# The order of the first units in a linear-attention and gated-MLP kernel: second head pair second, shared tail third

## The chip, the cores and the metric

The kernel runs on one core of a Trainium2 chip. The core has a matrix engine (TensorE, PE in the profile, with its weight loads as PEld), a vector engine (DVE), an activation engine (ACT), a general engine (GpSimd, POOL) and a queue engine that only starts transfers (SyncE, SP). Each runs its own instructions in order. Transfers are started on three queues: SP's, ACT's and POOL's; a transfer that changes the type (fp32 in memory, bf16 on chip) is started by POOL here. The metric is the device time of one execution in microseconds (us), lower is better.

## The reference

Eight batches, eight heads, 576 tokens, head size 64, 128 features per sign:

```python
def phi(x):
    proj = einsum('bhsd,df->bhsf', x, w_phi)
    proj = proj - max(abs(proj), axis=-1, keepdims=True)
    return concatenate([exp(proj), exp(-proj)], axis=-1)
q_p, k_p = phi(q), phi(k)
kv  = einsum('bhsf,bhsd->bhfd', k_p, v)
num = einsum('bhsf,bhfd->bhsd', q_p, kv)
den = einsum('bhsf,bhf->bhs', q_p, sum(k_p, axis=2))[..., None] + 1e-06
x = num / den                     # heads side by side: (8, 576, 512)
h = maximum(x @ w_in, 0.0)        # 1024 columns: u and v
v_n = (v - mean(v)) / sqrt(var(v) + 1e-06)
v_s = einsum('ts,bsd->btd', w_spatial, v_n) + b_spatial
out = (u * v_s) @ w_out
```

## The kernel before

**Units.** Of a batch's 576 tokens, 512 are the main part and 64 the tail. The tails of two batches (a group) share one 128-row tile. The attention is cut into 36 units: for each batch four *pairs* (two heads, 512 tokens each), and for each group one *tail* unit (both batches' tails, all heads). The list `units` (L558) fixes their order. For the first group it was: pair 1 of batch 0, tail, pairs 2, 3 and 4 of batch 0, then batch 1's four (called pairs 5 to 8 here).

**Stages of a unit.** `a_transpose` (L238) puts k and q in feature order through TensorE and DVE ("next"). `a_keys` (L260) projects k by w_phi, DVE takes the maximum of each row (`mk`, L268) and ACT the two exponentials (`kf`, L271). `a_scale` (L288) makes `em`, the exponentials of that maximum on ACT (L291), and POOL multiplies v with them (`vs`, L296, two instructions, and a cast at L298). For a tail unit `tail_scale` (L306) does that per batch (`vst`, L311, L313). `a_queries` (L273) does the same maximum for q (L282) and splits it in two bf16 parts (`mhl`, L285 and L286; on DVE for units 0 to 4, on POOL later). `a_max_t` (L315, "maxima") turns that part round, and `a_qfeat` (L325, "features") makes q's exponentials (`qf`, L355). `a_kv` (L358, "sums") forms kv of a pair from its own `kf` and `vs` and from the tail's, `a_num` (L381, "attention") the quotient, and `a_x_t` (L392, "out") its transpose.

**Steps.** `step(i)` (L622) issues, for each stage in the order of `ORDER` (L599), the unit whose number plus the stage's lag is i: `LAGS` in general, `FIRST` for the pairs of batch 0, `FT` for the first tail (L604 to L615). So step i does keys and queries of unit i, transposes of unit i + 1, sums of unit i - 2, attention of unit i - 3. When a batch's last pair is through "out", that batch's MLP (`b_tasks`, L581) goes to a queue of matmul tasks that `fill` (L608) puts between the stages. For batch 0 that is in step 7. The MLP's first spatial product (`b_s`, L508, matmul L513) needs the four normalised tiles `vn` (L454), written by POOL.

**Transfers and orders.** After each step the list `io`, filled by `at` (L664), issues transfers: batch 1's k and q (`load`, L97, POOL's queue) and v (`load_v`, L101, SP's queue) after step 1, MLP weights after steps 2 to 4, later batches' k and q after steps 4 and on. `load_tail` (L109) fetches a tail. A planner orders the instructions of each engine by their inputs and their place in the program; those wrapped in `pin` (L60) stay behind the instruction that was written last on their engine. A pinned instruction is shown under L61.

**Start.** Pair 1's k and q come as fp32 by SP's queue (`first`) and are cast on DVE. All other k and q come as bf16 by POOL's queue; pair 2's with `load("k", 0, 0, 2, 2)` and the same for q, after the tail's. Before the first exponentials ACT fills `vst` and `vnt` of the even and the odd groups and casts w_phi. `weights_with_max` (L228) builds `wm` on POOL (L230 to L232, four times three instructions), which is read from unit 10 on (L334); it is written after step 7 and not pinned.

Of the kernel before, what the change touches and what calls it, by code (L numbers as in the profile page):

```python
# [8 lines left out]
FP32 = mybir.dt.float32  # L9
# [7 lines left out]
def kernel(  # L17
# [106 lines left out]
    for i in range(2):  # L124
        nc.scalar.dma_start(out=wphi_f[i * D:(i + 1) * D, :], in_=w_phi)
    alloc(0)
    first = {}
    for x, t in (("k", k), ("q", q)):
        first[x] = s2.tile([P, 2, NB * D], FP32, tag="ob", name="first", bufs=6)
        pin(nc.sync.dma_start)(out=first[x], in_=main_ap(t, 0, 0, 2))  # L130
# [14 lines left out]
    for i in range(NM):  # L145
        for tiles, name in ((mhl, "mhl"), (mT, "mT")):
# [10 lines left out]
                                 scalar2=None, op0=ALU.mult)  # L157
    for x in ("k", "q"):
        pin(nc.vector.tensor_copy)(out=half_tile(x, 0, 0)[:, 0:2], in_=first[x])
    vst, vnt = [], []  # L160
    for i in range(2):
        t = cpool.tile([P, 2, 2, H, DA], BF16, name=f"vst{i}")
        pin(nc.scalar.copy)(out=t.rearrange("p b s h d -> p (b s h d)"), in_=zero.to_broadcast([P, 4 * H * DA]))
        vst.append(t)
        if i == 0:
            for y in range(2):
                r = slice(y * D, (y + 1) * D)
                pin(nc.scalar.copy)(out=wphi2[r, y * F:(y + 1) * F], in_=wphi_f[r, :])
        t = cpool.tile([P, 2, HALF], BF16, name=f"vnt{i}")
        for bl, row in ((0, TL), (1, 0)):  # L170
            pin(nc.scalar.copy)(out=t[:, bl, :], in_=ident[:, row:row + 1].to_broadcast([P, HALF]))
        vnt.append(t)
    load_v(0)
    for x in ("k", "q", "v"):
        load_tail(x, 0)
    load("k", 0, 0, 2, 2)
    load("q", 0, 0, 2, 2)
# [50 lines left out]
    def weights_with_max():  # L228
        for j in range(0, H, 2):
            nc.gpsimd.tensor_copy(out=wm[:, j, :], in_=wphi2[:, 0:F])  # L230
            nc.gpsimd.tensor_tensor(out=wm[:, j + 1, :], in0=wphi2[:, F:2 * F], in1=sel[:, j + 1, :], op=ALU.add)
            nc.gpsimd.tensor_copy(out=wm[D:D + 2 * H, j, :], in_=sel[0:2 * H, j, :])  # L232
# [5 lines left out]
    def a_transpose(u):  # L238
# [3 lines left out]
        for x, copy in (("k", nc.vector.tensor_copy if u["i"] < EK else nc.scalar.copy), ("q", nc.vector.tensor_copy)):  # L242
            pt = psum.tile([P, 4, P], BF16, tag="bank", name="pt")
            for j in range(4):
# [4 lines left out]
                nc.tensor.transpose(out=pt[:, j, :], in_=blk, identity=ident)  # L249
# [38 lines left out]
    def a_scale(u):  # L288
# [11 lines left out]
        else:  # L300
            d = gs[u["g"]]
            d["vs"], d["unit"], d["em"] = vst[u["g"] % 2], u, em
            for bl in range(2 if u["i"] > 1 else 1):
                tail_scale(u["g"], bl)
# [252 lines left out]
    for g in range(G):  # L557
        if g > 0:  # L558
            units.append(dict(pair=False, g=g, i=len(units)))
        for b in (2 * g, 2 * g + 1):  # L560
            for pj in range(NP):
                units.append(dict(pair=True, g=g, b=b, pj=pj, i=len(units)))
                if b == 0 and pj == 0:
                    units.append(dict(pair=False, g=g, i=len(units)))
# [169 lines left out]
```

## Time and profile before

| | |
|---|---|
| median of 5 runs | 284.14 us (282.28 to 284.51) |
| the profiled execution's own time | 284.51 us |
| its span in the profile | 282.7 us |
| PE busy | 258.7 us, 92% |
| DVE, ACT, POOL busy | 230.0, 223.2, 198.9 us |
| TensorE clock granted | 0.996 |

The span runs from the first to the last instruction; what lies around it makes 1.8 us. A line of the timeline has the start, the length, the engine, the line, the operation, the tile written and the tile read, the count, and in brackets how long the engine was idle before it and what ended that. "Busy" of several instructions counts overlaps once. The matmul's ends are modelled, and a matmul of 512 columns is shown with 0.38 us while the next starts after 0.22. A wait is put down to the event that came last by the profile, which can be an innocent one where several ended together.

### The profile page before, as it was taken

What the parts mean: (1) busy time and instruction counts of PE and PEld (TensorE: products, weight loads), DVE (VectorE), ACT (ScalarE), POOL (GpSimd) and SP (SyncE); (2) the same over time, 40 slices, a digit from 0 to 9 for tenths busy, and PEclk for the clock granted to TensorE, in tenths of its full rate; (3) what the DMA queues carried; (4) which work ended last, traced back from release to release, by engine and by line L of the source; (5) the groups of instructions that cost most, each with busy time, mean ns of one, the idle gap of its engine ahead of it and who ended that gap; (6) DMA issues with size and microseconds to landing.
All of it is one profiled execution on the core that took longest, in us unless ns stands there. A gap on an engine that the chain in (4) does not pass through costs nothing.

```text
span 282.7 us, 8167 instructions
## 1 busy us (share of the span) xinstructions
PE 258.7 (92%) x3042; PEld 172.3 (61%) x3042; DVE 230.0 (81%) x575; ACT 223.2 (79%) x504; POOL 198.9 (70%) x358
## 2 busy tenths in 40 slices
PE   3277899989999999999999999999999999999993
PEld 2046686767766577666666675666666765654441
DVE  5279999887999988998889989997889897566441
ACT  6739999997899997899889987899789977723601
POOL 8469999999758995799949984889548832420710
PEclk9999999999999999999999999999999999999998
DMA  6998999989877999979998999999665301121205
GB/s 178 208 179 103 200 210 235 145 152 189 96 95 166 176 200 203 172 184 214 154 143 126 220 262 127 202 190 235 95 122 132 85 3 48 66 77 38 111 3 185
DMA packets 85100, 41.91 MB, mean 148 GB/s; under 512 B 52098, under 2 KB 80450, under 8 KB 85060
## 3 DMA queue, kind: packets, MB, share of 16 engines
q1 hardware_dynamic: 57348, 29.90, 51.7%
q0 software_dynamic: 27552, 11.41, 36.4%
q8 instruction: 24, 0.39, 0.6%
q14 instruction: 16, 0.13, 0.2%
q10 hardware_dynamic: 160, 0.07, 0.1%
HBM read 32.85 MB, written 9.44 MB: 150 GB/s over the span
## 4 chain that ended last, share of the span: by engine, by line
PE 62%; ACT 10%; DMA 9%; POOL 7%; DVE 7%; issue 3%; POOLq 0%; ACTq 0%; DVEq 0%
PE ps L513 9%; PE pv L437 9%; PE po L538 8%; PE pu L492 7%; PE ps L256 6%; DMA q_tl<-in_q_dram 4%; PE pv L368 4%; ACT kf L271 4%; PE pn L388 4%; DMA k_bf<-in_k_dram 3%; PE pq L334 3%; PE ps L514 2%; ACT qf L355 2%; DVE stats L440 2%; DVE mk L268 2%
## 5 line engine op out<-in xcount | busy, mean ns | idle before, releaser
L271 ACT ACTIVATE kf<-ps 128x512 bf16<-128x512 f32 x144 | 76.1, 633 | 11.6 <-DVE mk L268 11.1
L296 POOL TENSOR_TENSOR vs<-v_f,em 128x512 bf16<-128x512 f32 x64 | 65.5, 1045 | 21.3 <-ACT em L291 16.4
L355 ACT ACTIVATE qf<-pq 128x512 bf16<-128x512 f32 x128 | 66.6, 619 | 9.0 <-PE pq L334 8.5
L268 DVE TENSOR_REDUCE mk<-ps 128x4 f32<-128x512 f32 x72 | 47.7, 677 | 1.3 <-PE ps L256 0.4
L282 DVE TENSOR_REDUCE mq<-ps 128x4 f32<-128x512 f32 x62 | 39.8, 680 | 2.5 <-PE ps L256 2.2
L513 PE MATMUL ps<-w_spT,vn 128*128 128x512 bf16 x128 | 33.2, 379 | 0.5 <-POOL vn L454 0.4
L440 DVE BATCH_NORM_STATS2 stats<-vr 128x6 f32<-128x512 bf16 (+1 forms) x40 | 26.7, 684 | 7.2 <-ACT vr L439 6.9
L516 DVE TENSOR_TENSOR uT<-ps,uT 128x512 bf16<-128x512 f32 x32 | 22.0, 686 | 12.9 <-PE ps L514 12.8
L538 PE MATMUL po<-w_out_bf,uT 128*128 128x512 bf16 x128 | 32.3, 379 | 0.0
L492 PE MATMUL pu<-xT,w_in_bf 128*128 128x512 bf16 x128 | 32.1, 379 | 0.0
L437 PE MATMUL pv<-w_in_bf,xT 128*128 128x512 bf16 x128 | 31.5, 379 | 0.1
L439 ACT ACTIVATE vr<-pv 128x512 bf16<-128x512 f32 (+1 forms) x40 | 23.5, 615 | 7.3 <-PE pv L437 6.1
L368 PE MATMUL pv<-vs,kf 128*128 128x66 bf16 x512 | 24.6, 194 | 1.3 <-ACT kf L271 1.3
L454 POOL TENSOR_SCALAR vn<-vr,rs 128x512 bf16<-128x512 bf16 x32 | 24.4, 770 | 1.1
L379 DVE TENSOR_TENSOR x<-pn,rc 128x256 bf16<-128x256 f32 x64 | 24.9, 417 | 0.3
L388 PEld LDWEIGHTS <-qf 128*128 128x128 bf16 x512 | 20.2, 97 | 7.8 <-ACT qf L355 1.2
L368 PEld LDWEIGHTS <-kf 128*128 128x128 bf16 x512 | 22.1, 98 | 3.5 <-issue 2.3
L494 ACT ACTIVATE uT<-pu 128x512 bf16<-128x512 f32 x32 | 19.6, 639 | 4.9 <-PE pu L492 3.2
L388 PE MATMUL pn<-kv,qf 128*128 128x66 bf16 x512 | 21.9, 193 | 1.0 <-ACT qf L355 1.0
L541 ACT COPY ob<-po 128x512 f32<-128x512 f32 x18 | 11.0, 610 | 14.9 <-PE po L538 8.6
L370 PE MATMUL pv<-vst,kf 128*128 128x66 bf16 x128 | 21.2, 191 | 0.8 <-POOL vst L313 0.8
L311 POOL TENSOR_TENSOR vst<-v_tl,em 64x512 bf16<-64x512 f32 x16 | 16.3, 1039 | 7.7 <-ACT em L291 7.4
(128 smaller groups left out, 568.0 us busy)
## 6 DMA issues: line engine op xcount, KB each, us to landing
out_dram<-ob SPq DMA_DIRECT2D x32, 256.0 KB, 2.5
v_f<-in_v_dram SPq DMA_DIRECT2D x12, 512.0 KB, 6.1
k_bf<-in_k_dram POOLq DMA_DIRECT2D x15, 256.0 KB, 6.2
q_bf<-in_q_dram POOLq DMA_DIRECT2D x15, 256.0 KB, 6.7
v_f<-in_v_dram SPq DMA_DIRECT2D x2, 1024.0 KB, 12.3
qt<-qT_b SPq DMA_DIRECT2D x24, 64.0 KB, 4.2
v_tl<-in_v_dram SPq DMA_DIRECT2D x8, 128.0 KB, 5.1
w_in_bf<-in_moe_w_in_dram POOLq DMA_DIRECT2D x2, 512.0 KB, 7.6
```

What stands on the lines that cost most here:

```text
L268: nc.vector.tensor_reduce(out=u["mk"][:, hs], in_=pk, axis=AX.X, op=ALU.max, apply_absolute_value=True)
L271: nc.scalar.activation(out=u["kf"][:, s, hs, :], in_=pk, func=AF.Exp, bias=0.0, scale=sc)
L282: nc.vector.tensor_reduce(out=mq[:, 4 * half:4 * half + 4], in_=pq, axis=AX.X, op=ALU.max, apply_absolute_value=True)
L296: nc.gpsimd.tensor_tensor(out=vs[:, s, :, 0:D], in0=st[u["b"]]["v"][:, pj * H:(pj + 1) * H, :], in1=em[:, s, :].unsqueeze(2).to_broadcast( ...
L355: nc.scalar.activation(out=qf[:, s], in_=pq, func=AF.Exp, bias=0.0, scale=sc)
L368: nc.tensor.matmul(out=pv[:, hh, s, :], lhsT=u["kf"][:, s, 4 * hh + c, :], rhs=u["vs"][:, s, 4 * hh + c, :], start=(c == 0), stop=False)
L388: nc.tensor.matmul(out=pn[:, pos, :], lhsT=u["qf"][hh][:, s, pos, :], rhs=d["kv"][:, 2 * u["pj"] + hh, s, :], start=(s == 0), stop=(s == 1))
L437: nc.tensor.matmul(out=pv[r], lhsT=lhs(kc), rhs=w_in_bf[:, kc, HALF:DFF], start=(kc == 0), stop=(kc == KC - 1))
L440: nc.vector.bn_stats(out=stats[r], in_=dst[r])
L492: nc.tensor.matmul(out=pu, lhsT=w_in_bf[:, kc, dc * P:(dc + 1) * P], rhs=d["xT"][:, kc, :], start=(kc == 0), stop=(kc == KC - 1))
L513: nc.tensor.matmul(out=ps, lhsT=d["vn"][:, sp, cs], rhs=w_spT[:, sp, 0:T0], start=(sp == 0), stop=False)
L538: nc.tensor.matmul(out=po[r], lhsT=lhs(dc), rhs=w_out_bf[:, dc, :], start=(dc == 0), stop=(dc == KC - 1))
```

## The change

In the first group the units are now pair 1, pair 2, tail, pair 3, pair 4. Pair 2's k and q come as fp32 by SP's queue right behind pair 1's and are cast by two pinned POOL instructions; the two POOL loads for them are gone. POOL's loads of pairs 3 and 4 are issued behind these casts. v of batch 0 comes in two halves, with the tail's k, q and v between them. w_phi comes by one transfer that reads the weights twice, in place of two transfers.

The steps 0 to 3 follow lists of their own (`START`): features of pairs 1 and 2 come one step after their queries (before: two), sums three (before: two), attention four (before: three). The transposes of the tail and of pair 3 stand in their own step ("here", pinned) and not in the step before.

The zeros of `vst` of the odd groups are now a DVE memset, placed ahead of the first casts, and the constant rows of `vnt` of the odd groups two POOL copies after step 1; ACT casts w_phi first, then fills `vnt` and `vst` of the even groups. Batch 1's first k and q loads are issued after step 0 (before: 1). `wm` is built in two halves, pinned, after steps 6 and 7. The instructions of `tail_scale` are pinned, and the second batch's half of the first tail is scaled after step 5 (before: 4).

```diff
-    for i in range(2):
-        nc.scalar.dma_start(out=wphi_f[i * D:(i + 1) * D, :], in_=w_phi)
+    nc.scalar.dma_start(out=wphi_f, in_=bass.AP(tensor=w_phi.tensor, offset=w_phi.offset,
+                                                ap=[[0, 2], [F, D], [1, F]]))
...
-    for x, t in (("k", k), ("q", q)):
-        first[x] = s2.tile([P, 2, NB * D], FP32, tag="ob", name="first", bufs=6)
-        pin(nc.sync.dma_start)(out=first[x], in_=main_ap(t, 0, 0, 2))
+    for h0 in (0, 2):
+        for x, t in (("k", k), ("q", q)):
+            first[x, h0] = s2.tile([P, 2, NB * D], FP32, tag="ob", name="first", bufs=6)
+            pin(nc.sync.dma_start)(out=first[x, h0], in_=main_ap(t, 0, h0, 2))
...
+    vst = [cpool.tile([P, 2, 2, H, DA], BF16, name=f"vst{i}") for i in range(2)]
+    pin(nc.vector.memset)(vst[1], 0.0)
     for x in ("k", "q"):
-        pin(nc.vector.tensor_copy)(out=half_tile(x, 0, 0)[:, 0:2], in_=first[x])
-    vst, vnt = [], []
-    for i in range(2):
-        t = cpool.tile([P, 2, 2, H, DA], BF16, name=f"vst{i}")
-        pin(nc.scalar.copy)(out=t.rearrange("p b s h d -> p (b s h d)"), in_=zero.to_broadcast([P, 4 * H * DA]))
...
-    load_v(0)
+        pin(nc.vector.tensor_copy)(out=half_tile(x, 0, 0)[:, 0:2], in_=first[x, 0])
+    vnt = [cpool.tile([P, 2, HALF], BF16, name=f"vnt{i}") for i in range(2)]
+
+    def fill_vnt(i, copy):
         for bl, row in ((0, TL), (1, 0)):
+            pin(copy)(out=vnt[i][:, bl, :], in_=ident[:, row:row + 1].to_broadcast([P, HALF]))
+
+    for y in range(2):
+        r = slice(y * D, (y + 1) * D)
+        pin(nc.scalar.copy)(out=wphi2[r, y * F:(y + 1) * F], in_=wphi_f[r, :])
+    fill_vnt(0, nc.scalar.copy)
+    pin(nc.scalar.copy)(out=vst[0].rearrange("p b s h d -> p (b s h d)"), in_=zero.to_broadcast([P, 4 * H * DA]))
+    load_v(0, 0)
     for x in ("k", "q", "v"):
         load_tail(x, 0)
-    load("k", 0, 0, 2, 2)
-    load("q", 0, 0, 2, 2)
+    load_v(0, 1)
+    for x in ("k", "q"):
+        pin(nc.gpsimd.tensor_copy)(out=half_tile(x, 0, 0)[:, 2:4], in_=first[x, 2])
     load("k", 0, 1)
     load("q", 0, 1)
...
-    def weights_with_max():
-        for j in range(0, H, 2):
+    def weights_with_max(n):
+        for j in range(4 * n, 4 * n + 4, 2):
...
+                (pin(nc.tensor.transpose) if u["i"] in LATE else nc.tensor.transpose)(out=pt[:, j, :], in_=blk, identity=ident)
...
-            for bl in range(2 if u["i"] > 1 else 1):
+            for bl in range(2 if u["g"] else 1):
...
-                if b == 0 and pj == 0:
+                if b == 0 and pj == 1:
                     units.append(dict(pair=False, g=g, i=len(units)))
...
+    LATE = (2, 3)
+    START = [[(what, 0) for what in names.split()] for names in (
+        "keys next queries", "keys maxima queries features", "maxima features here keys queries",
+        "maxima here keys queries features sums next")]
+    HEAD = dict(next=-1, maxima=1, features=1, sums=3, attention=4, out=4)
...
     def lag(u, what):
-        return (FT if u["i"] == 1 else FIRST if u["pair"] and u["b"] == 0 else LAGS).get(what, 0)
+        if what == "next" and u["i"] in LATE:
+            return NU
+        if u["i"] < 5:
+            return (HEAD if u["i"] < 2 else FIRST if u["pair"] else FT).get(what, 0)
+        return LAGS.get(what, 0)
...
-    at(1, load, "k", 1, 0)
-    at(1, load, "q", 1, 0)
+    at(0, load, "k", 1, 0)
+    at(0, load, "q", 1, 0)
+    at(1, fill_vnt, 1, nc.gpsimd.tensor_copy)
...
-    at(4, tail_scale, 0, 1)
+    at(5, tail_scale, 0, 1)
...
-    at(7, weights_with_max)
+    at(6, weights_with_max, 0)
+    at(7, weights_with_max, 1)
```

## The prediction

> **What bounds the kernel now.** I read the busy time by stage first, to see where TensorE is not the limit.
>
> ```profile
> 0.00:8.00 8.00, 3.08 (x16) 1.81 (x16) 5.01 (x19) 5.71 (x7) 7.23 (x16) 1.00 0.74 189
> 8.00:20.00 12.00, 4.54 (x29) 3.16 (x29) 5.01 (x12) 6.44 (x15) 5.57 (x15) 1.00 1.29 204
> 20.00:44.00 24.00, 20.45 (x312) 16.90 (x311) 23.17 (x66) 21.83 (x53) 23.75 (x35) 1.00 1.11 170
> 44.00:70.00 26.00, 24.68 (x322) 18.04 (x322) 21.60 (x61) 23.57 (x56) 24.51 (x43) 1.00 1.25 175
> 70.00:250.00 180.00, 178.21 (x2174) 119.05 (x2172) 161.24 (x394) 156.08 (x360) 131.10 (x240) 1.00 0.91 149
> ```
>
> Columns: stage, its length, then busy us of PE, PEld, DVE, ACT, POOL, the granted clock, DMA, GB/s. From 70 to 250 us PE is busy 178.21 of 180: a delay or gain on PE ahead of 70 reaches the end whole, nothing later swallows it. The first 20 us hold only 7.6 us of PE work. From 20 to 44 POOL is full (23.75 of 24) and DVE nearly (23.17); from 44 to 70 POOL still is (24.51 of 26). So the opening has two clocks: the first loads set when work starts, and POOL sets how fast it is handed to PE.
>
> Then the PE timeline, for who starts late:
>
> ```profile
> 6.04 1.01 PE L256 MATMUL ps<-wphi,kT 128*128 128x256 bf16 x4 [0.27 <-ACT wphi L61]
> ...
> 13.13 0.58 PE L249 MATMUL pt<-ident,k_tl 128*128 128x128 bf16 x4 [5.22 <-DMA k_tl<-in_k_dram]
> ...
> 15.96 0.58 PE L249 MATMUL pt<-ident,q_tl 128*128 128x128 bf16 x4 [2.25 <-DMA q_tl<-in_q_dram]
> ...
> 24.37 0.61 PE L256 MATMUL ps<-wphi,kT 128*128 128x256 bf16 x4
> ...
> 71.19 1.03 PE L513 MATMUL ps<-w_spT,vn 128*128 128x512 bf16 x4
> ```
>
> After pair 1's projections (6.04) PE waits 5.22 and 2.25 us for the tail's k and q; pair 2 follows at 19.35, and 24.37 is pair 3's key projection. 71.19 is batch 0's first spatial matmul, which needs all four `vn`.
>
> The POOL timeline, for where it is free and what it delivers:
>
> ```profile
> 6.70 0.77 POOL L61 DMA_DIRECT2D q_bf<-in_q_dram  x1
> ...
> 12.37 2.04 POOL L296 TENSOR_TENSOR vs<-v_f,em 128x512 bf16<-128x512 f32 x2 [3.50 <-DMA v_f<-in_v_dram]
> ...
> 17.19 0.28 POOL L232 COPY wm<-sel 16x128 bf16<-16x128 bf16 x1
> 19.97 2.04 POOL L311 TENSOR_TENSOR vst<-v_tl,em 64x512 bf16<-64x512 f32 x2 [2.50 <-ACT em L291]
> ...
> 55.57 0.21 POOL L298 CAST vs<-em 128x32 bf16<-128x32 f32 x1
> ...
> 67.19 2.28 POOL L454 TENSOR_SCALAR vn<-vr,rs 128x512 bf16<-128x512 bf16 x3
> ```
>
> POOL idles 3.50 and 2.50 us, and from 19.97 runs with no gap worth naming through `vs` of pair 8 (ends 55.8) to the last `vn` (ends 69.47). PE's load of those weights starts at 71.1, so POOL has 1.65 us of slack there. The chain of waits puts 8.65 us at 39.68 on a k transfer; the matmul it ends in (L437) reads `xTt`, which DVE wrote at 47.98, so I read this as that copy and not as a load.
>
> Last, the third pair's q transfer, which POOL issues at 6.70:
>
> ```profile
> q_bf<-in_q_dram POOLq DMA_DIRECT2D x1, 256.0 KB, 15.3
> ```
>
> It lands at 22.0.
>
> **The change, part by part.** *Loads of pair 2.* Two 128 KB POOL loads go (0.79 + 0.72 us of issue), two fp32 loads join SP's queue ahead of v. On SP, k lands at 0.73 + 2.8 = 3.5 and q at 1.25 + 3.4 = 4.65; the queue then moves about 0.25 MB per us, so 0.26 MB more each gives 6.1 and 7.2. By the old rows it was 17.2 and 18.7. SP's later issues (v in halves, tail v, batch 1's v) slip by the two new issues of 0.5 us and by 0.5 MB, and the extra v issue; v of heads 0 to 3 stands at 1.57 MB of its queue, just where all of v stood, so it lands by 12.3 at the latest.
>
> *Casts on POOL.* No such row exists. A 128x128 copy takes 0.292, a 128x32 cast 0.208: 0.0009 per element, so 512 elements are 0.63; the 512-element TENSOR_SCALAR of L454 is 0.77. I take 0.7 (ends 0.63 and 1.05, the two-input row). They run at 6.1 to 8.0, in the old idle before 12.37, so they cost nothing by themselves. But pair 3's and 4's k and q loads are queued behind them: issue of the last moves from 6.70 to 8.8, done 9.6. If that cover is gone, 3 us at most pass to these loads.
>
> DVE's own cast rows of this shape are 0.54 and 0.43, so casts left there would take 1.4 us off POOL where it idles and put 1.0 on DVE; the sum is the same by either. The Trainium skill, GPSIMD Engine Reference, section 4.1, speaks against the change here: it sends elementwise work to VectorE, and its 3.1 gives 512 elements at best 769 ns on GpSimd.
>
> *Pair 3's data.* POOL's queue loses two loads ahead of these. At about 0.08 MB per us while SP's queue also moves (the rows of 13 to 18 us), 0.26 MB less is 3 us, less the later issue: 22.0 becomes about 20.0. Ends: 18.7, the landing of the load whose place it takes; 24.9, the old 15.3 us after issue at 9.6. From landing to key projection is 0.6 (18.76 to 19.35 for pair 2), so pair 3 starts at 20.6 in place of 24.37: 3.8 earlier. Pairs 1 and 2 and the tail before it fit: ACT has two exps sets more (2.1 each, pair 2's keys and queries) plus pair 1's queries, ready by 17, and the tail's at 17 to 19.4.
>
> *From pair 3 to the fill.* The same units, with the same DVE work, follow in the same steps; sums and numerators of pairs 1 and 2 keep one per step, moved by one. I keep 3.5 of 3.8 for the fuller DVE queue (bound: 4.8, ACT's start of pair 3's exps, 25.77 against 21).
>
> *ACT and DVE setup.* ACT loses one 1.95 and one 1.13 copy set; its first exps (9.95) start after w_phi (5.99), `vnt` 1.14 and `vst` 1.95, at 9.1; pair 1's `em` follows 2.2 later at 11.3. DVE gains a memset of 1,056 words: the 576-word one took 0.54, so 1.0, of which 0.66 is idle time before the first cast; the 0.35 left is covered by the wait for w_phi at 6.04. One DMA for w_phi instead of two: 4.4 us either way, up to 0.3 (PE's wait) to gain, counted as 0.
>
> *POOL's sum.* `vs` of pair 1 starts at 11.3 (ends: 11.3 by `em`, 12.4 by v). Behind it: itself 2.2; all that ran from 19.97 to 55.80, 35.8 (the moved loads and the tail's second half are in it, only in another order); `wm`, no longer in the idle stretch, 4 x (0.292 + 0.424 + 0.284) = 4.0; `vnt` of the odd groups, two copies of 0.63, 1.3 (end: 1.5 by 0.77). Together 43.3: ends at 54.6, with 0.4 of waiting for pair 3's `em`, 55.0. Before: 55.8. So POOL, which had 6 us of idle time, wins only 0.8, because 5.3 us of work were put in the full stretch. With the slack of 1.65 PE can be at L513 2.5 us earlier, not 3.5. Nothing POOL does in between binds sooner: the second half of the tail now stands behind pair 5's maxima, its end near 39 to 40.5, and sums that need it ran at 44.61, or 41.1 when 3.5 earlier.
>
> **Sum:** min(3.5, 0.8 + 1.65) = 2.5 us. The profiled run took 284.51 (span 282.7), so 282.0 against itself; its time is 0.37 above the median of the runs, 284.14, so 281.6 against that.
>
> Splitting v is a second place to weigh. The 1024 KB loads land in 12.3 at the median, the 512 KB ones in 6.1: no loss per byte, so I count nothing. v's second half is first used by pair 3's `vs` at about 23, so even some us more would stay hidden. The Trainium skill, DMA: Bandwidth & Descriptors, section Bandwidth, speaks against it: it wants batches of 1 MiB and more; an estimate by the fixed 2 us per transfer that the page fits for POOL's path would land that half 2 us later.
>
> **The rivals.** *POOL does not bind* (0.17). If the planner puts `wm` or the next group's tail products (4.5 us, ahead of the first root) behind `vn`, the whole 3.5 to 4.5 stays: about 280.2. For it: `wm` is first read at 80.15 and pair 10's sums at 78.94. Against: the pinned order puts both halves of `wm` behind loads of steps 6 and 7, ahead of `vn`.
>
> *POOL takes all of it* (0.15). v lands at 12.4, casts and `vnt` at their upper ends: 12.4 + 43.6 + 0.4 = 56.4, 0.6 later than before; with the slack 1.0 is left: 283.1, no change that can be told. For it: 12.37 was released by v and the bytes ahead of half of v are the same. Against: POOL's queue has nothing but the tail until 8.
>
> *Pair 3's loads late: slower* (0.18). At 24.9 its keys are at 25.5 and its `em` at 28.3; POOL, free at 22.9, idles 5.4 in its full stretch. 54.6 + 5.4 = 60.0, 4.2 late, less 1.65: +2.6, 286.7. It turns at an idle of 1.2 + 1.65 = 2.85 us, that is at a landing near 22.4. For it: the issues stand behind two casts that wait for SP's queue, and batch 1's loads now compete. Against: 0.26 MB less in that queue. A start as the diff has it, with no effect on the order of these engines, I exclude: nothing else feeds pair 2.
>
> **How the numbers follow.** My case 0.50, the rivals 0.17, 0.15, 0.18. 0.5% is 1.4 us, what a measurement here can tell from nothing. My own case spans 1.0 to 3.5 of gain (280.6 to 283.1), 0.43 of it beyond 1.4. Faster: 0.43 + 0.17 = 0.60. Same: 0.07 + 0.14 = 0.21. Slower: 0.18 + 0.01 = 0.19. The range takes in the second gain up to 4.8 (279.3) and the late load up to 1.5 of its 2.6 (285.6); outside lie 0.03 and 0.14.
>
> **What would show it.** Right: no wait of PE for tail loads; `first` of pair 2 landed by 7.5; pair 3's L256 near 20.6; POOL without a gap from 11 to 69; `vs` of pair 8 ending near 55; PE waiting for `vn` 1 us before its first L513, near 68.7. Wrong: a POOL gap between 20 and 30 (late loads), L513 below 67.5 (POOL not binding), or a stage after 70 whose PE idle has grown, for there the offset would not carry.

## The result, and the profile after

The changed kernel takes 285.62 us at the median against 284.33 for the one before: ratio 1.005, 95% interval 1.0038 to 1.0061. It is slower by half a per cent, where 281.6 and a gain were predicted. The ratios leave out executions in a slower state of the chip, here two of the changed kernel's 43 (291.79 and 908.68 us). The profiled execution took 285.31 (span 283.4) against 284.51 (span 282.7): 0.8 in the profile, 1.3 between the medians. Single executions of the kernel before scatter from 282.28 to 286.19, so one profile tells where time goes, and only the runs tell which kernel is faster. Lines of the code stand two further down than before: L256 is now L258, L513 is L515, L514 is L516, L454 is L456, L437 is L439, L538 is L540.

Busy time by stage after, in the columns of the first view before:

```profile
0.00:8.00 8.00, 1.21 (x8) 0.79 (x9) 4.36 (x17) 1.88 (x4) 4.56 (x12) 1.00 0.82 185
8.00:20.00 12.00, 9.27 (x66) 6.67 (x65) 8.80 (x20) 11.78 (x24) 8.76 (x13) 1.00 1.31 240
20.00:44.00 24.00, 19.28 (x316) 16.63 (x317) 23.13 (x64) 18.89 (x47) 21.92 (x35) 0.93 1.19 160
44.00:70.00 26.00, 24.67 (x313) 17.85 (x309) 21.25 (x58) 23.57 (x56) 24.11 (x48) 1.00 1.22 181
70.00:250.00 180.00, 177.32 (x2152) 117.88 (x2150) 160.37 (x392) 154.82 (x358) 133.50 (x243) 1.00 0.91 149
```

PE does 9.27 us of work between 8 and 20 where it did 4.54: the empty stretch was indeed filled. The work that was put there ran at a lower rate: four products of 128x256 took 1.06 us as late as 13.50 and 0.61 from 18.37 on (before: 1.04 as late as 20.28), though the clock column shows 1.00. But ACT, with 5.71 us of work in the first 8 before, has 1.88 now, and POOL, which was full from 20 to 44 (23.75), is idle for 2.1 us of it.

The PE timeline after, at the tail, at pair 3 and at batch 0's first spatial products:

```profile
8.02 1.01 PE L258 MATMUL ps<-wphi,kT 128*128 128x256 bf16 x4 [1.16 <-ACT wphi L61]
...
18.37 0.61 PE L258 MATMUL ps<-wphi,kT 128*128 128x256 bf16 x4 [0.30 <-DVE kT L253]
18.81 0.60 PE L258 MATMUL ps<-wphi,qt 128*128 128x256 bf16 x4
21.95 0.23 PE L319 MATMUL pt<-ident,mhl 128*128 128x128 bf16 x1 [2.54 <-DVE mhl L288]
22.02 0.39 PE L61 MATMUL pt<-ident,k_bf 128*128 128x128 bf16 x4
22.24 0.39 PE L61 MATMUL pt<-ident,q_bf 128*128 128x128 bf16 x4
22.92 0.61 PE L258 MATMUL ps<-wphi,kT 128*128 128x256 bf16 x4 [0.29 <-DVE kT L253]
...
71.21 0.39 PE L515 MATMUL ps<-w_spT,vn 128*128 128x512 bf16 x1 [0.36 <-POOL vn L456]
71.96 0.39 PE L515 MATMUL ps<-w_spT,vn 128*128 128x512 bf16 x1 [0.36 <-POOL vn L456]
72.19 0.38 PE L516 MATMUL ps<-w_spT,vnt 128*128 128x512 bf16 x1
```

The waits for tail loads are gone. Pair 3 begins at 22.92 (before 24.37), and not for want of data: its transposes (22.02) are pinned behind the tail's maxima (21.95), and these wait 2.54 us for DVE. The last two lines of L515 wait for `vn` tile by tile, so the first product of the bias rows (L516) is at 72.19. Before it was at 72.05:

```profile
72.05 0.38 PE L514 MATMUL ps<-w_spT,vnt 128*128 128x512 bf16 x1
```

The lead is spent by then.

The POOL and the ACT timeline after:

```profile
6.74 0.61 POOL L61 CAST k_bf<-first 128x512 bf16<-128x512 f32 x1 [2.21 <-DMA first<-in_k_dram]
7.81 0.61 POOL L61 CAST q_bf<-first 128x512 bf16<-128x512 f32 x1 [0.46 <-DMA first<-in_q_dram]
...
13.12 2.04 POOL L298 TENSOR_TENSOR vs<-v_f,em 128x512 bf16<-128x512 f32 x2 [3.23 <-ACT em L293]
...
26.32 2.04 POOL L298 TENSOR_TENSOR vs<-v_f,em 128x512 bf16<-128x512 f32 x2 [1.63 <-ACT em L293]
...
58.01 0.21 POOL L300 CAST vs<-em 128x32 bf16<-128x32 f32 x1
...
69.63 2.28 POOL L456 TENSOR_SCALAR vn<-vr,rs 128x512 bf16<-128x512 bf16 x3
```

```profile
6.08 1.28 ACT L61 ACT_TABLE_LOAD   x1 [6.08 <-DMA wphi_f<-in_w_phi_dram]
7.37 0.60 ACT L61 CAST wphi<-wphi_f 64x128 bf16<-64x128 f32 x2
8.00 1.14 ACT L61 COPY vnt<-ident 128x512 bf16<-128x512 bf16 x2
9.04 1.95 ACT L61 COPY vst<-zero 128x2112 bf16<-128x2112 bf16 x1
10.89 2.05 ACT L273 ACTIVATE kf<-ps 128x512 bf16<-128x512 f32 x4
```

POOL starts `vs` of pair 1 at 13.12, later than before (12.37), waits 1.63 at pair 3, ends `vs` of pair 8 at 58.2 (before 55.8) and the last `vn` at 71.91 (before 69.47). ACT's first instruction is now the w_phi cast, and the load of its function table, 1.28 us, which ran at 1.95 before, stands with it behind the w_phi transfer. ACT's timeline before:

```profile
1.95 1.28 ACT L61 ACT_TABLE_LOAD   x1 [1.95 <-issue]
3.24 1.95 ACT L61 COPY vst<-zero 128x2112 bf16<-128x2112 bf16 x1
5.10 0.29 ACT L61 CAST wphi<-wphi_f 64x128 bf16<-64x128 f32 x1
...
9.95 2.05 ACT L271 ACTIVATE kf<-ps 128x512 bf16<-128x512 f32 x4
```

After L516 the two executions run in step: from the second product of the bias rows (74.52 before, 74.50 after) to 262 us they are within 0.04. Two differences come after that, both in the last batch. ACT's last `vr` starts 0.28 later, and the end of the span comes 0.38 later after the last output products. The timeline of all engines there, its ACT lines and SP's last, first of the kernel before:

```profile
261.78 0.60 ACT L439 ACTIVATE vr<-pv 128x512 bf16<-128x512 f32 x1 [1.13 <-POOL rs L448]
262.64 0.60 ACT L439 ACTIVATE vr<-pv 128x512 bf16<-128x512 f32 x1 [0.27 <-PE pv L437]
...
278.94 1.11 SPq L553 DMA_DIRECT2D out_dram<-ob  x2
```

and of the changed kernel:

```profile
261.81 0.60 ACT L441 ACTIVATE vr<-pv 128x512 bf16<-128x512 f32 x1 [1.13 <-POOL rs L450]
262.96 0.60 ACT L441 ACTIVATE vr<-pv 128x512 bf16<-128x512 f32 x1 [0.55 <-PE pv L439]
...
279.25 1.11 SPq L555 DMA_DIRECT2D out_dram<-ob  x2
```

The last issue ends at 280.05 before and at 280.36 after, the spans at 282.7 and 283.4: 2.65 us are left in the one and 3.04 in the other. Spans are printed to 0.1 us, so such lengths up to the end are good to 0.05. So the span's 0.7 is 0.14 at L516, -0.1 on the way to 262, and 0.28 and 0.38 at the end; the last 0.1 of the profiled 0.8 lies around the span.

### The profile page after: what moved, and what is told of

It is laid out like the page before. It is cut to its first block, busy times and chain, and to the rows that moved or that the text cites. A ratio compares the mean times of both kernels' runs of the same rounds, so it can differ in the third digit from the quotient of the medians.

```text
span 283.4 us, 8170 instructions
## 1 busy us (share of the span) xinstructions
PE 259.6 (92%) x3042; PEld 173.3 (61%) x3042; DVE 232.0 (82%) x576; ACT 220.4 (78%) x501; POOL 199.6 (70%) x360
## 4 chain that ended last, share of the span: by engine, by line
PE 66%; DVE 14%; ACT 10%; POOL 3%; issue 3%; DMA 2%; POOLq 0%; ACTq 0%; DVEq 0%
PE pv L439 11%; PE ps L515 9%; PE po L540 9%; PE ps L258 8%; PE pu L494 6%; PE pv L370 5%; DVE mk L270 4%; PE pn L390 4%; ACT kf L273 4%; PE pq L336 3%; PE ps L516 2%; ACT qf L357 2%; POOL vn L456 2%; DVE stats L442 2%; DMA wphi_f<-in_w_phi_dram 2%
## 5 line engine op out<-in xcount | busy, mean ns | idle before, releaser
L515 PE MATMUL ps<-w_spT,vn 128*128 128x512 bf16 x128 | 33.8, 380 | 1.6 <-POOL vn L456 1.4
L518 DVE TENSOR_TENSOR uT<-ps,uT 128x512 bf16<-128x512 f32 x32 | 21.9, 686 | 14.5 <-PE ps L516 14.5
L540 PE MATMUL po<-w_out_bf,uT 128*128 128x512 bf16 x128 | 32.3, 379 | 0.0
L439 PE MATMUL pv<-w_in_bf,xT 128*128 128x512 bf16 x128 | 31.5, 379 | 0.2 <-ACT kf L273 0.2
L456 POOL TENSOR_SCALAR vn<-vr,rs 128x512 bf16<-128x512 bf16 x32 | 24.4, 771 | 1.1
```

The source lines that it names most:

```text
L439: nc.tensor.matmul(out=pv[r], lhsT=lhs(kc), rhs=w_in_bf[:, kc, HALF:DFF], start=(kc == 0), stop=(kc == KC - 1))
L515: nc.tensor.matmul(out=ps, lhsT=d["vn"][:, sp, cs], rhs=w_spT[:, sp, 0:T0], start=(sp == 0), stop=False)
L540: nc.tensor.matmul(out=po[r], lhsT=lhs(dc), rhs=w_out_bf[:, dc, :], start=(dc == 0), stop=(dc == KC - 1))
```

## The experiments

Theories. *POOL binds, ACT starts late* (mine, mended): POOL's work as summed, but its start and its wait at pair 3 were set wrongly. *The order holds pair 3*: its place on PE behind the tail's maxima, not its load. *The end*: the two small losses after 262 us have nothing to do with the opening.

**The start on ACT.** The fill goes first, so that the table load and 1.95 us of copies run while w_phi is on its way.

```diff
+    pin(nc.scalar.copy)(out=vst[0]..., in_=zero...)
     for y in range(2):
         pin(nc.scalar.copy)(out=wphi2[...], in_=wphi_f[r, :])
     fill_vnt(0, nc.scalar.copy)
-    pin(nc.scalar.copy)(out=vst[0]..., in_=zero...)
```

> The changed kernel, but ACT's first instruction is again the fill of vst (even groups), which needs no transfer, and the two casts of w_phi come behind it. Theory A (start): ACT's table load waited 6.08 us for w_phi because it stands in front of ACT's first instruction; now it loads at about 2 us, the casts of w_phi end near 6.7 in place of 7.97, pair 1's vs on POOL starts near 11 in place of 13.12, pair 3's keys near 21.1 (its q lands at 20.5) in place of 22.92, the last vn ends near 70.1 in place of 71.91. Time 1.8 us below the changed kernel, about 283.8, no longer slower than before. Theory B (only POOL's total of work counts, not when it starts): vn and the time move by less than 0.5 us. Theory C (the loss sits in the last 20 us of the kernel or in the clock dip at 24 to 28 us): nothing moves in the time though the start is earlier.

284.69 in the profile; 285.02 by the runs, ratio 1.0038 (1.0013 to 1.0063). `vs` of pair 1 came 2.0 us sooner (11.13, where it waited 1.01 for v), the tail's keys 0.44 (17.93), pair 3's too (22.48 for 22.92), L516 at 71.65. The start is repaired, and only 0.44 of its 2.0 us reached pair 3: something behind it held.

**wm on POOL, early.** Unpinned and after step 7, as before; it then ran at 10.3 to 14.5, in POOL's idle stretch. The second kernel has the fill first as well.

```diff
-            pin(nc.gpsimd.tensor_copy)(out=wm[:, j, :], in_=wphi2[:, 0:F])
+            nc.gpsimd.tensor_copy(out=wm[:, j, :], in_=wphi2[:, 0:F])
...
-    at(6, weights_with_max, 0)
+    at(7, weights_with_max, 0)
```

> The changed kernel, but the twelve POOL instructions that build wm are not pinned and written after step 7 as before, so that the planner puts them behind pair 4's q load, from about 9.9 us, where POOL idles. Theory A: 4.0 us leave POOL's full stretch, of which 0.9 comes back as pair 1's vs starts at 14 and not at 13.12, and that is taken from the wait of 1.63 ahead of pair 3's vs; the last vn ends near 68 in place of 71.91, PE does not wait for it and keeps its lead of 1.2 us over the kernel before; L516 first near 71.0; 1.2 us below the changed kernel, about 284.4. Theory B gives the same here. Theory C: no change in the time.

> Both edits. Theory A: pair 3's keys near 21.1, vs of pair 1 near 13.9 (wm ahead of it), the last vn near 67, L516 first near 69.1 in place of 72.19: 3 us below the changed kernel, about 282.5, 0.6% below the kernel before. Theory B: as with wm alone, 284.4. Theory C: no change.

284.93, ratio 1.0018 (0.9992 to 1.0044), and 285.07, 1.0027 (1.0000 to 1.0053). The wait for `vn` was gone in both (`vn` ends 69.85 and 69.15), as POOL's theory says, but L516 came at 72.72 and 72.02. `wm` ran ahead of the tail's products: `vst` at 23.16 in place of 21.76, pair 4's keys at 27.95 in place of 26.81, and pair 8's at 47.77 and 47.08 in place of 45.89. In these traces PE gave back what POOL won. Not all of that is the work of `wm`: in the first trace the granted clock was 0.74 from 20 to 24 us and 0.50 from 24 to 32, and that execution, at 285.87, lies 0.9 above its kernel's median. In the second the clock was 1.00 and 0.94 up to 28 us, and pair 4's keys still came 4.7 after pair 3's (23.01 and 27.72), against 3.65 with the fill first alone (22.48 and 26.13). By the runs the first kernel is 0.7 below the changed one, with intervals that just overlap, so whether relieving POOL at this place pays is not settled.

**The start on ACT, in the old order.** The kernel before with w_phi cast first.

```diff
+    for y in range(2):
+        pin(nc.scalar.copy)(out=wphi2[...], in_=wphi_f[r, :])
     vst, vnt = [], []
     for i in range(2):
...
-        if i == 0:
-            for y in range(2):
-                pin(nc.scalar.copy)(out=wphi2[...], in_=wphi_f[r, :])
```

> The kernel before with one part of the change alone: ACT casts w_phi first, ahead of its fills. Theory A: ACT's table load moves from 1.95 to about 5.7 and pair 1's keys from 6.04 to about 7.7, but PE then waits for the tail's k until 13.1 and POOL idles 2.5 us ahead of 19.97, so the old order covers all of it: within 0.3 us of the kernel before. Rival: a late first exponential costs its 1 to 2 us in the old order too, near 285.7, and the whole loss of the changed kernel is this.

285.22, ratio 1.0014 (0.9983 to 1.0045), the profile 283.72. Here ACT's table load waited until 4.01, the first exponentials came at 11.72 in place of 9.95 and `vs` of pair 1 at 13.94 in place of 12.37; yet pair 2's keys were at 18.63 (19.35) and the first product of the bias rows at 71.32 (72.05). So in the trace the late start costs nothing: pair 2 waits for the tail's loads behind it. The runs alone leave room for more, as the interval reaches 1.0045. Filling that wait took the cover away from ACT's start.

**Pair 3 ahead of the tail's maxima.**

```diff
-        "maxima here keys queries features sums next")]
+        "here keys maxima queries features sums next")]
```

> The changed kernel with one word moved: in step 3 the transposes and keys of pair 3 stand ahead of the maxima of the tail, not behind them. Theory D (order): pair 3 starts at 22.92 and not at the landing of its q, 20.5, because its transposes stand behind the tail's maxima on PE, which wait for DVE's split of the tail's maximum (2.54 us of wait ahead of L319); with the order turned its keys start near 21.2, its vs on POOL near 24.7 in place of 26.32, the last vn ends near 70.3, L516 first near 70.6 in place of 72.19: 1.6 us below the changed kernel, about 284.0. Theory A (the late start of ACT sets pair 3): its keys stay at 22.5 or later and the time within 0.5 us of the changed kernel.

285.07, ratio 1.0009 (0.9986 to 1.0032), the profile 284.14. On PE:

```profile
18.95 0.39 PE L61 MATMUL pt<-ident,k_bf 128*128 128x128 bf16 x4
20.96 0.40 PE L61 MATMUL pt<-ident,q_bf 128*128 128x128 bf16 x4 [1.62 <-DMA q_bf<-in_q_dram]
21.20 0.60 PE L258 MATMUL ps<-wphi,kT 128*128 128x256 bf16 x4
```

Now the load of q sets pair 3, at 21.20 as expected, 1.72 sooner than in the changed kernel. This shows that the order held it. Of the 1.72, 1.15 arrived at L516 (71.04), where PE again waited for `vn`.

**The second group's tail products behind vn.** Its two pairs of `vst` instructions, 4.6 us of POOL, go from ahead of the first `vn` to behind step 10.

```diff
-            for bl in range(2 if u["g"] else 1):
+            for bl in range(0 if u["g"] == 1 else 2 if u["g"] else 1):
...
+    for bl in range(2):
+        at(10, tail_scale, 1, bl)
```

> The changed kernel, but the tail products of the second group (4.6 us of POOL ahead of the first vn) are written after step 10 in place of step 9. The opening stays as it is. If POOL's sum costs the changed kernel its lead, the last vn ends near 67.3, PE does not wait for it, L516 first stands 24.9 after pair 8's keys as in the kernel before, near 70.8 in place of 72.19: 1.4 us below the changed kernel, about 284.2. If the wait for vn only hides another (a product of the MLP that comes no sooner), the time moves by less than 0.4 us.

284.60, ratio 1.0008 (0.9982 to 1.0034), the profile 284.76. The wait for `vn` is gone (`vn` ends at 67.8), and from pair 8's keys (46.18) to L516 (71.11) it is 24.93, as in the kernel before; the changed kernel took 26.30. That is the price of POOL: 1.37 us.

**All three** (fill first, pair 3 first, tail products later).

> ACT's fill first, pair 3 ahead of the tail's maxima, the second group's tail products after step 10. If start, order and POOL's sum are the three places of the loss, pair 3's keys near 21.1, pair 8's near 44, no wait for vn, L516 first near 69.0: 3.2 us below the changed kernel, about 282.4 and 0.7% below the kernel before. If the time of the last 20 us of the kernel or the clock takes it back, it stays above 284.

L516 at 69.56, the profile 283.71; by the runs 284.91, ratio 1.0004 (0.9978 to 1.0029). L516 comes 2.5 us sooner than in the kernel before. Of that 1.75 is left at 262 us, the two losses of the end take 0.66, and the span is 1.1 shorter. The other 0.75 went between the fourth and the fifth product of the bias rows (78.7 and 105.9 before), in batch 1. The kernel with the later tail products alone loses 0.28 there (0.94 to 0.66), and the one with pair 3 first alone loses nothing (1.17 to 1.13), so the later tail products have a part in it; what PE met there is not shown. The profiled execution is 1.2 below its kernel's median; by the medians the kernel is level with the one before.

**The late wm alone, in the old order.** In the kernel before, pinned, in halves after steps 6 and 7.

```diff
-    at(7, weights_with_max)
+    at(6, weights_with_max, 0)
+    at(7, weights_with_max, 1)
```

> The kernel before with one part of the change alone: wm is built in two pinned halves after steps 6 and 7. POOL's sum: 4.0 us join the full stretch, the last vn ends near 73.4 in place of 69.47, of which 1.65 is slack: L514 first near 74.4 in place of 72.05, 2.3 us slower than before, about 286.6. If POOL is not what L513 waits for, within 0.5 us of before.

285.74, ratio 1.0055 (1.0025 to 1.0086). PE waits for three `vn` tiles in a row:

```profile
71.53 0.39 PE L513 MATMUL ps<-w_spT,vn 128*128 128x512 bf16 x1 [0.74 <-POOL vn L454]
72.28 0.39 PE L513 MATMUL ps<-w_spT,vn 128*128 128x512 bf16 x1 [0.35 <-POOL vn L454]
73.03 0.39 PE L513 MATMUL ps<-w_spT,vn 128*128 128x512 bf16 x1 [0.36 <-POOL vn L454]
```

This one part, without the new order, costs the old kernel as much as the whole change does. POOL as the bound, the centre of the prediction's sum, is shown. The last `vn` ended at 72.97, 3.5 later than before, and the first product of the bias rows came at 73.25, 1.2 later: POOL had 2.3 us to spare there, and not the 1.65 that the expectation took over from the prediction.

**The end: the last transfer.** In the traces SP's and ACT's transfers take eight completion semaphores in turn. Counted from 0 in the order of the first eight, the last two output transfers use numbers 6 and 7 before, 0 and 1 after, since the change has two such transfers more in all. Three kernels shift the turn late in the program, by the number of pieces in which v of the last batches comes: two more in the kernel before, and two fewer or six more in the changed one.

```diff
-                for y in range(2):
-                    at(i - AB + 1 + 2 * y, load_v, u["b"], y)
+                for y in range(2 if u["b"] < 6 else 1):
+                    at(i - AB + 1 + 2 * y, load_v, u["b"], y if u["b"] < 6 else None)
```

> The kernel before; only v of batch 7 comes in four quarters in place of two halves, so two transfers more stand on SP's queue late in the kernel, and every later transfer uses the semaphore two places on among the eight that SP's and ACT's transfers take in turn. The opening is untouched. If that turn causes the loss at the end (in all kernels of the new order the last output copy to the end of the span is 5.86 to 5.91, in the three of the old order 5.46 to 5.53): 5.87, and 0.38 us more by the profile, 284.7 by the runs. If the loss belongs to the new order of the units in some other way: 5.48, and the time of the kernel before. The 28th to the 29th spatial matmul of the bias rows (14.38 to 14.40 in the old order, 14.65 to 14.69 in the new): 14.66 if it hangs on the same, else 14.39.

> The changed kernel; only v of batches 6 and 7 comes in one transfer each in place of two, so the last transfers use the same semaphores as in the kernel before. If the turn of the semaphores causes the loss at the end: last output copy to end of span 5.48 in place of 5.86, and the time 0.4 to 0.7 us lower, 285.0 by the runs. If not: 5.86, and 285.6.

> The changed kernel; only v of batches 5, 6 and 7 comes in four quarters each, six transfers more, so the turn of the eight semaphores stands as in the kernel before (two more and six more make eight). If the turn counts: 5.48 at the end, as with two fewer, 285.0 by the runs. If the number of transfers counts, or their bytes in flight: 5.86 or more, and 285.6 or above.

From the end of the last issue to the end of the span, and from the last output products (L538 or L540) to it:

| | last two on | issue to end | products to end | median | ratio to before |
|---|---|---|---|---|---|
| before | 6, 7 | 2.65 | 5.48 | 284.33 | |
| before, two more | 0, 1 | 3.08 | 5.90 | 284.81 | 1.0015 (0.9983 to 1.0048) |
| after | 0, 1 | 3.04 | 5.86 | 285.62 | 1.0050 (1.0038 to 1.0061) |
| after, two fewer | 6, 7 | 2.68 | 5.51 | 284.95 | 1.0020 (0.9996 to 1.0044) |
| after, six more | 6, 7 | 2.69 | 5.52 | 284.86 | 1.0020 (1.0003 to 1.0036) |

The turn sets it, not the number of transfers: two fewer and six more give the same. Why the end is longer on 0 and 1 is not shown. The 28th to the 29th product of the bias rows stayed at 14.70 and 14.68 in the changed kernel and at 14.39 in the old one, so that loss is another thing.

> The three edits together (fill of the tail's weighted v first on ACT, pair 3's transposes ahead of the tail's maxima, the second group's tail products later), and v of batches 6 and 7 in one transfer each. If the end hangs on the turn of the semaphores: the profile 0.4 to 0.7 below that of the three edits, near 283.2, and 284.3 by the runs, the kernel before or a little less. If not: 283.7 and 284.9.

283.89, ratio 0.9990 (0.9971 to 1.0008); 5.53 at the end. L516 was at 70.81 in this profile and not at 69.56, so the profiled time was 284.47. Pair 3's q landed late (21.4), which put its keys 0.44 later (21.71 for 21.27). The other 0.8 is there by pair 4's keys (26.84 for 25.57), in a stretch where the granted clock was 0.89 and 0.69 (20 to 24 and 24 to 28 us) and 1.00 in the kernel with all three.

**The end: ACT's last vr.** The changed kernel has four ACT instructions fewer (three fills and a transfer). In the kernel just measured, four small unused copies on ACT, where it waits for w_phi, put every later instruction back in its place; a second kernel, further down, has two.

```diff
+    idle = cpool.tile([P, 8], BF16)
+    for n in range(4):
+        pin(nc.scalar.copy)(out=idle, in_=ident[:, 0:8])
```

> The kernel of three edits with two transfers fewer, and four copies of 128 x 8 on ACT between the fill of the tail's weighted v and the w_phi casts, where ACT idles 1.28 us for the w_phi transfer. They compute nothing that is used. They put every later ACT instruction four places on, as many as the change took out (three fills and one w_phi transfer). If the 0.28 us lost between the 28th and the 29th spatial product of the bias rows (14.39 in the old order, 14.68 in the new) come from where ACT's instructions stand in its program, then 14.39 here, and the fetch of instructions that the transfers show after 263 us moves to 260 to 262 as in the kernel before; 283.6 by the runs. If they come from the order of the units: 14.68, and 283.9. Nothing moves in the opening.

283.47, ratio 0.9985 (0.9962 to 1.0007). The 28th to the 29th product: 14.39. The last three `vr` on ACT, with four copies:

```profile
259.45 0.60 ACT L444 ACTIVATE vr<-pv 128x512 bf16<-128x512 f32 x1 [0.55 <-PE pv L442]
260.90 0.60 ACT L444 ACTIVATE vr<-pv 128x512 bf16<-128x512 f32 x1 [0.85 <-POOL rs L453]
261.76 0.60 ACT L444 ACTIVATE vr<-pv 128x512 bf16<-128x512 f32 x1 [0.27 <-PE pv L442]
```

The pause of 0.28 has not gone: it stands at the `vr` two places earlier (0.55 in place of 0.27), where the next one waits for POOL anyway (0.85 in place of 1.13).

**Pair 3's loads ahead of the casts**, alone and with the four copies.

```diff
+    load("k", 0, 1)
+    load("q", 0, 1)
     for x in ("k", "q"):
         pin(nc.gpsimd.tensor_copy)(out=half_tile(x, 0, 0)[:, 2:4], in_=first[x, 2])
-    load("k", 0, 1)
-    load("q", 0, 1)
```

> The kernel of three edits with two transfers fewer; pair 3's and pair 4's first k and q loads are issued by POOL ahead of the two casts, as soon as the tail's are, so q of pair 3 leaves at about 5.5 in place of 9.57. If pair 3 now hangs on its load (it waits 2.21 us for q, keys at 21.71), its keys come 1.3 to 2.2 us sooner, at 19.5 to 20.4, and the fill too: first spatial product near 69.3, 282.6 by the runs. If the transfer is bound by bytes and lands at 20.5 whenever it is issued: keys 21.2, and 283.9. The casts come 0 to 0.8 us later, which pair 2's keys (10.16) show.

> Both edits of the two runs before this one. The sum of the two gains if they are independent: 282.3 by the runs where each does what it should; 283.9 where neither does.

283.68, ratio 0.9986 (0.9963 to 1.0008), and 283.31, ratio 0.9970 (0.9943 to 0.9998). The loads left at 5.29 and PE no longer waits for them: the transposes of q follow those of k at once, and the keys (21.35, 20.12) wait 1.21 us for DVE's copy. Against its sibling with late loads pair 3 gains 0.4 and 0.2, less than the 1.3 to 2.2 expected, as DVE is next. The second of these beats the kernel before, narrowly, and the changed kernel by 2.3 us between the medians. It is the best of eighteen kernels that were measured, and its interval just misses 1, so the lead over the kernel before may be luck.

> The kernel before, with only its setup changed: the fill of the odd groups' weighted v is a DVE memset, the constant rows of the odd groups' vnt are two DVE copies, and w_phi comes by one transfer; so ACT has four instructions less, as in the changed kernel, and the order of the units is the old one. If the 0.28 us hang on the place of ACT's instructions: 14.68 between the 28th and the 29th spatial product of the bias rows, 284.7 by the runs. If they belong to the order of the units: 14.39, 284.4. At the opening ACT is free 3 us sooner, but pair 2 waits for the tail's loads as before, so its first spatial product stays within 0.7 us of 72.0. One ACT transfer less: the last output copy to the end of the span stays at 5.48 or 5.86, by the turn of the semaphores.

In the old order, four ACT instructions fewer by the setup alone:

```diff
+        if i == 0:
             pin(nc.scalar.copy)(out=t..., in_=zero...)
+        else:
+            pin(nc.vector.memset)(t, 0.0)
...
-            pin(nc.scalar.copy)(out=t[:, bl, :], in_=ident...)
+            pin(nc.vector.tensor_copy if i else nc.scalar.copy)(out=t[:, bl, :], in_=ident...)
```

283.82, ratio 1.0002 (0.9975 to 1.0028), and 14.37: no loss. So four instructions fewer do not make it by themselves; the order has a part in what stands at the place where ACT pauses. The setup's move costs nothing in the old order. Its 159 transfers leave the last two on numbers 5 and 6, with 2.8 us from the last issue to the end: of the three places seen, only 0 and 1 are long.

**The two ends and the start mended, the opening as changed.** The changed kernel with two transfers fewer and the four copies, here ahead of the w_phi casts; then the best kernel with two copies in place of four.

> The changed kernel with its opening order as it is, but without the two losses at the end: v of batches 6 and 7 in one transfer each, and four copies of 128 x 8 on ACT, unused, which here stand ahead of the w_phi casts and so are ACT's first instructions. At the end: 14.39 between the 28th and the 29th product of the bias rows (14.69 in the changed kernel) and 5.5 from the last output copy to the end (5.86). At the start the table load no longer stands behind the w_phi transfer: w_phi casts at 6.1 in place of 7.37, pair 1's keys near 6.8 in place of 8.02, as with the fill first, where 0.5 us of that reached pair 8. By that the profile is 285.3 - 0.3 - 0.4 - 0.5 = 284.1. If the two end losses and the start are the whole of the loss: not slower than the kernel before by the runs, 284.0 to 284.5. If the opening itself loses: 285.0 or more.

284.88, ratio 1.0007 (0.9985 to 1.0029). In the one trace of it the mean granted clock was 0.751, so only ACT's first lines are read there (table load at 1.88, w_phi casts at 6.47), and the two lengths at the end were not seen in this kernel. Its interval lies below that of the changed kernel. Without these three the changed kernel is level with the one before; its opening wins nothing and loses nothing that can be told.

> The kernel with copies and loads, with two idle copies in place of four: ACT's later instructions stand two places sooner. If the loss in the last batch's MLP hangs on where the fetch of ACT's instructions falls, it shows one of the two values, 14.39 or 14.68, and nothing between; if it hangs on the number in proportion, 14.53. The opening is the same: pair 3's keys at 20.1, first spatial product at 69.6, and 283.3 by the runs, or 283.6 with 14.68.

283.91, ratio 0.9979 (0.9955 to 1.0004), and 14.60, neither of the two values. The ACT timeline says why:

```profile
259.93 1.17 ACT L444 ACTIVATE vr<-pv 128x512 bf16<-128x512 f32 x2 [1.42 <-POOL var L454]
```

The pause is now at the `vr` between the two earlier cases (1.42 in place of 1.13), and its successor follows without the usual 0.27, so 0.21 of 0.28 is left. With four fewer, two fewer and none, the pause moves one `vr` at a time: it belongs to a place in ACT's instruction stream. What ACT does there is open. The one instruction transfer on queue 14 in this stretch moves with it. It starts 0.8 us after the start of the late `vr` in the changed kernel (263.77 and 262.96) and in the one with early loads alone (262.78 and 261.99), 0.65 after it with four copies (260.10 and 259.45) and 0.63 with two (260.56 and 259.93). So both mark one place in the stream. But the transfer comes after the pause, so ACT did not wait for it, and in the kernel before it starts at 260.18, just behind a `vr` (260.05) that is not late.

## Why the prediction was wrong

*What bounds the kernel*: right for the changed kernel, whose offset on PE held level from 74 to 262 us. But "a delay or gain on PE ahead of 70 reaches the end whole" was read from windows that stop at 250, and in the kernel with all three edits 0.75 of a lead of 2.5 was gone by 106 us. In the changed kernel 0.28 and 0.38 us were added in the last 20 us, by the place of ACT's instructions and the turn of the semaphores. No step of mine priced instructions and transfers beyond the stage in which they stand. These two are 0.66 of the span's 0.7.

*Loads of pair 2, casts*: right. k and q landed for casts at 6.74 and 7.81 (predicted 6.1 and 7.2), 0.61 each (0.7). The Trainium skill (GPSIMD Engine Reference, 3.1) has 769 ns for 512 elements, as the measured best of a loop unrolled four times; the casts undercut it, and the measurement decides. Its section 4.1, which the prediction sets against the casts, calls two-input work about twice slower there, and one-input work roughly line-rate; these casts have one input. Splitting v, which the prediction counted at nothing, against the Trainium skill (DMA: Bandwidth & Descriptors, section Bandwidth: batches of 1 MiB and more), cost nothing that shows: no POOL product of batch 0 in the changed kernel waits for v. With the fill first, v's first half bound `vs` of pair 1 at 11.13, inside the predicted 12.3.

*Pair 3's data*: the transfer was right, 11.4 us after its issue at 9.14, so 20.5 (20.0). The step failed at "From landing to key projection is 0.6 … so pair 3 starts at 20.6": it started at 22.92, 2.3 later, because PE had the tail's maxima in front of it, waiting for DVE. I had checked that ACT's work fitted, and not what stands ahead of a pinned transpose on PE. The run with pair 3 first gave 21.20.

*From pair 3 to the fill* ("3.5 of 3.8"): about right. Pair 3 to pair 8 took 22.97 against 22.75 before, so 1.23 of the 1.45 us was kept.

*ACT and DVE setup*: wrong by 1.8 us. "first exps (9.95) start after w_phi (5.99), vnt 1.14 and vst 1.95, at 9.1" left out the table load, which the timeline before has at 1.95, ahead of a transfer's landing, and which moved behind it; and w_phi landed at 6.08, 5.35 after its issue where 4.4 was taken, so its casts were at 7.37. Exps started at 10.89, `vs` of pair 1 at 13.12 in place of 11.3. I also took up to 0.3 to gain at PE's first keys; they came 1.98 later.

*POOL's sum*: 43.3 us was right. From 13.12 it gives 56.4, with the measured wait of 1.63 at pair 3 58.05, and 58.2 was measured; predicted was 55.0, by 1.82 of late start and 1.23 more of waiting than the 0.4 I allowed. The kernel with the late `wm` alone and the one with the later tail products show the mechanism from both sides.

*Slack*: 1.65 was mis-sized. It compares the last `vn` with PE's first load of such weights; the four products take the tiles one after the other, and the last tile is read some 0.7 later. Where PE waited for `vn`, the first product of the bias rows came 0.28 after the last `vn` ended (72.19 and 71.91 here, 73.25 and 72.97 with the late `wm`); before it came 2.58 after (72.05 and 69.47). That is 2.3 of slack: POOL, 2.44 late, cost L516 0.14, and all of the lead. So the sum with measured terms is about nothing, where I had min(3.5, 0.8 + 1.65) = 2.5.

*Rivals*: the result of the opening is that of *POOL takes all of it*, but neither its late v nor upper ends did that: ACT's start and the order on PE did. *Pair 3's loads late* did not happen; the POOL gap between 20 and 30 that was to show it came (1.63) from pair 3's `em`, so that sign did not tell the two apart. *POOL does not bind* is refuted by the waits for `vn`. What made it slower and not equal was in none.

Part of the difference between the medians stays unexplained: 1.3 by the runs and 0.8 by the profiles, which are one execution each. With the end and the start mended the ratio is 1.0007, so by the medians these causes hold most of it; the interval, up to 1.0029, leaves room for a rest. One rival is the granted clock. Among the executions behind the ratios, 19 of 146 of the kernel before have a mean clock under 0.995, with a median of 285.18, and the other 127 have 284.14; in the changed kernel it is 40 of 42. Against it: the other two of the changed kernel, at 0.999 and 1.000, took 286.01 and 285.82, and the mended kernel is level although ten of its eleven are under 0.995. So the clock does not make the half per cent by itself; whether it has a share is open.

## What to carry to other kernels

When a wait is filled, list on each engine what stood behind it under its cover: here ACT's table load and pair 3's place on PE were free only as long as PE waited for the tail. Price a stall at the reader's last tile and not its first, and give a lead only the smallest of the limits that follow it. Half a per cent can hang on small things at the end, here on which semaphore the last transfer takes and where an instruction falls in its stream; compare the last 20 us of both traces before the opening is blamed.

## What the runs showed of the hardware

The load of ACT's function table waits for the data of ACT's first instruction: it started at 6.08 (changed kernel) and 4.01 (w_phi first in the old order) where the first instruction reads w_phi, and at 1.88 to 1.95 where it reads none of a transfer's data.

The end of the kernel after the last issue was 2.65 to 2.69 us with the last two transfers on semaphores 6 and 7, and 3.04 to 3.08 on 0 and 1, each good to 0.05.

In the new order ACT's pause of 0.28 us moved with the number of instructions ahead of it, one `vr` for every two copies.

The granted TensorE clock fell to about half for some us soon after the opening in the traces of most kernels of the new order. In the changed kernel:

```profile
20.00:24.00 4.00, 1.75 (x17) 1.40 (x18) 3.34 (x10) 1.77 (x6) 3.88 (x7) 0.94 1.33 178
24.00:28.00 4.00, 3.40 (x47) 2.96 (x45) 3.79 (x11) 2.25 (x6) 2.37 (x4) 0.63 1.13 162
```

The kernel before has 1.00 in both. All five traces of the old order have 1.00 from 0 to 44 us, and so have three of the new: pair 3 first, early loads alone, and two copies. The old order is not free of it: some executions of the kernel before have a mean clock as low as theirs (0.99 and less).

Time was lost with it in the opening. With the same opening, pair 4's keys came 3.89, 4.44 and 4.21 us after pair 3's where the clock was down there (the changed kernel, two fewer, six more) and 3.64 where it was 1.00 (later tail products); from pair 4 to pair 8 all four took 19.0 to 19.1. In the three with the lower clock POOL set the first product of the bias rows (72.1 to 72.3), so this cost did not come through.
